# A long convolution and a cosine-gated MLP on one core: sines of tables, stores of matrices and a copy moved in their queues

## The chip, the cores and the metric

One core of a Trainium2 chip. It has five engines that run their own instruction queues in order: TensorE (PE; its weight loads are listed as PEld), VectorE (DVE), ScalarE (ACT), GpSimd (POOL) and SyncE (SP, which here only issues DMAs). They wait for each other by semaphores, and an instruction that waits holds up everything behind it on its own engine. The metric is device microseconds of one execution; the kernel before takes 3782.1 us (median of four runs, 3780.03 to 3782.74).

## The reference

```
B, S, D = 4, 12480, 128
h_filt = (relu(pos_emb @ w1) @ w2) * exp(-0.01 * pos)[:, None]
u = x * v
y = causal convolution of u with h_filt along S      # by FFT of length 2*S
X = (x * y).reshape(B*S, D)                           # 49920 rows
h = X @ w_in                                          # 128 -> 2048
out = (h * cos(h)) @ w_out                            # 2048 -> 128
```

All is float32 (w_in and w_out come as 64-bit floats and are converted on the chip).

## The kernel before, in words

**Convolution.** It is a transform of length M = 96 x 120, in two steps each way, by matmuls with tables of cosines and sines. For each batch there are four stages: f1 (64 units of two channels: matmuls against the table `c1`, L404, then copies out of PSUM, L420 to L422 and L414, done for some units by ACT and for the others by DVE, after a fixed share); f2 (48 units of two frequencies: matmuls with a matrix `w`, L445, then the product with the filter's transform `h` on DVE, L464 or L468/L470, whose sums POOL takes, L471); i1 (64 units: matmuls with the table `cs`, L476, a copy on ACT, L484, and a sum and a difference on DVE, L486); i2 (30 groups of four matrices `tm`, L501, then a product with x on DVE, L506, which is stored to `zd`).

The filter goes through f1 as well (evictions L431 to L436 and L412/L414), and through f2 together with batch 0 (`f2_both_units`; its matmuls are L448 and L451). In that stage the matrix w(j) of each unit is made from the tables `even` and `tw_w`: ACT writes one term to a PSUM bank (L291), DVE adds the other (L293). SP stores it to `wd` (L613), since the later batches load it again; the filter's product h(j) is made by ACT (L624) and stored to `hd` (L626) for the same reason. w has two buffers, h three. `units` (L524) gives the order: in unit j come w(j+1), then the matmuls of unit j, then h(j-1), its store and the product of unit j-1.

**Tables.** `inverse_tables` (L252) makes ten pieces of the tables `cs`, `rows` and `tw_t` beside the filter's f1. POOL works out the arguments (L200 to L217), ACT takes their sine (L226). A sine is issued when four arguments are waiting, the rest after the last; then SP stores the three tables (L270). The loop at L860 advances this by one piece at every fifth step of f1 (a unit of f1 has two steps).

**Conversions.** `beside` (L870) runs the conversion of the 64-bit weights beside f1 of batch 0 (w_in) and beside i1 of batch 0 (w_out), eight pieces each, one at every 14 steps. A piece takes DVE (L133, L141, L151), POOL (L135, L137, L147, L156) and ACT (L144, L146). In i1, `some_groups` also makes the matrices of six of the 30 groups, one matrix at every fifth step; at its end it starts the first i2 (`next(backs[0])`), which makes the first group `tm`.

**Groups.** A matrix of a group is made by `turn` (L282): ACT writes a term (L291), and either DVE adds the other (L293) or ACT makes it too, in a `spare` (L296), and POOL adds (L297). Of a group's four, the first two go by DVE and the last two by POOL, with one spare. The six groups of `some_groups` go by POOL alone.

**MLP.** From 344 us on, 98 tiles of 512 columns run, each in 16 steps. A step is `moe_up` (L737 matmul to a bank `ph`, L740 ACT `a`, L743 DVE `k`, L746 POOL `f`), one step later `moe_act` (L751 ACT Sin `cs`, L753 DVE `gt`), and four steps later `moe_down` (L762, which adds up 16 steps in the bank `acc`). After the sixteenth, `moe_evict` copies the sums to `ot` on ACT (L768); `ot` goes back through transposes (L126), is copied to `ob` (L777) and stored. The convolutions of the other batches, with i2 of batch 0 first, are laced between the steps by costs written in the code (L551 to L554), until all of `zd` is there, at about 2960 us; `acc` has one bank till then.

Of the kernel before, what the change touches and what calls it, by code (L numbers as in the profile page):

```python
# [2 lines left out]

# [27 lines left out]
def kernel(  # L31
# [220 lines left out]
    def inverse_tables(pool):  # L252

        t = Tables(pool, nc.gpsimd, 4)
        part = t.whole([P, 1], [[1, 1]], channel_multiplier=1, name="part")
# [11 lines left out]
                           eighths=slice(H - 1, N2, H))  # L267
        t.finish(len(t.waiting))
        for kept, made in ((csd, cs), (rowsd, rows), (twd, tw_t)):
# [182 lines left out]

    def f2_product(pool, ps, h, k1, whole):

# [11 lines left out]
        for r, op in ((0, ALU.subtract), (1, ALU.add)):  # L466
            if not whole:
                nc.vector.tensor_tensor(y[:, r], uu[:, 0], h[:, r], op=ALU.mult)  # L468
                yield
                nc.vector.tensor_tensor(t[:, r], uu[:, 1], h[:, 1 - r], op=ALU.mult)  # L470
            nc.gpsimd.tensor_tensor(y[:, r], y[:, r], t[:, r], op=op)  # L471
            yield
# [130 lines left out]

    def f2_both_units(bank):

        with tc.tile_pool(name="both", bufs=2) as pool:
            ws = {}

            def before(j):
                ws[j] = pool.tile([KE, 2, N2], F32, name="w")  # L610
                for i in range(2):
                    make_w(ws[j][:, i, :], 2 * j + i, half=bank)
                nc.sync.dma_start(wd[j, :, :, :], ws[j][:, :, :])  # L613

            def mm(j, ps, i):
                if i == 0:
                    ps = bank(), bank()
                for filt in range(2):
                    f2_mm(ps[filt], ws[j], 2 * j, i, filt=filt == 1)
                return ps  # L620

            def after(j, ps):
                h = pool.tile([N2, 2, CB, 4], F32, name="h", bufs=3)
                nc.scalar.activation(h[:, :, :, :].rearrange("p r b j -> p (r b j)"),  # L624
                                     ps[1][0:N2, :], AF.Copy, scale=1.0 / M)
                nc.sync.dma_start(hd[j, :, :, :, :], h[:, :, :, :])  # L626
                yield from f2_product(pool, ps[0], h, 2 * j, True)

            yield from units(N1 // 2, F2_STEPS, before, mm, after, 4, ahead=1)

# [10 lines left out]

    def make_group(pool, g, t, summed, bufs=1):

        for i, n2 in enumerate(n2s(g)):
            if i < G - summed:
                make_t(t[:, i, :, :], n2)
            else:
                spare = pool.tile([N1, 2, R], F32, name="spare", bufs=bufs)
                make_t(t[:, i, :, :], n2, spare=spare[:, :, :])
            yield  # L650
        nc.sync.dma_start(td[g, :, :, :, :], t[:, :, :, :])

    def some_groups(pool):
        for g in SOME:
            t = pool.tile([N1, G, 2, R], F32, name="some", bufs=2)
            yield from make_group(pool, g, t, G, bufs=2)
        next(backs[0])

# [135 lines left out]
    with tc.manual_schedule():  # L794
        with tc.tile_pool(name="psum", bufs=8, space=PSUM) as psum, \
                ExitStack() as first:
            def bank():
                return psum.tile([P, BANK], F32, name="ps")
# [59 lines left out]
            with tc.tile_pool(name="tables", bufs=1) as pool:  # L858
                sines = inverse_tables(pool)
                for i, _ in enumerate(f1):  # L860
                    if i % 5 == 0:
                        next(sines, None)
                for _ in sines:
                    pass

# [3 lines left out]

            def beside(units, pieces, more=lambda pool: iter(())):  # L870
                with tc.tile_pool(name="convert", bufs=1) as pool:
                    convert, other = convert_units(pool, pieces), more(pool)
                    for i, _ in enumerate(units):
                        if i % 14 == 0:
                            next(convert, None)
                        elif i % 5 == 0:
                            next(other, None)
                    for _ in [*convert, *other]:
                        pass

            beside(f1_units(bank, slots[0:R, :, :, :], 0.55),
                   [(wind[:, c], w) for c, w in in_pieces])
            lpool = ctx.enter_context(tc.tile_pool(name="late", bufs=1))
            cs = third_table(lpool)
            nc.sync.dma_start(cs[:, :, :], csd[:, :, :])
            for _ in f2_both_units(bank):
                pass
# [12 lines left out]
            nc.sync.dma_start(w_in_sb[:, :], wind[:, :])  # L900
            beside(i1_units(bank), [(w_out_sb[:, c, :], w) for c, w in out_pieces], some_groups)

# [28 lines left out]
        for i in range(len(steps) + LAG):  # L931
            if i < len(steps):
# [5 lines left out]
                hidden[i] = moe_up(mpool, n, c)  # L938
            if 0 <= i - 1 < len(steps):
                gates[i - 1] = moe_act(mpool, *hidden.pop(i - 1))  # L940
            if i >= LAG:
                pn, pc = steps[i - LAG]
                moe_down(pn, pc, gates.pop(i - LAG))
                if pc == NFC - 1:
                    ots[pn] = moe_evict(mpool, pn)
            if i < len(steps):

# [39 lines left out]
```

## Time and profile before

| | |
|---|---|
| median of four runs | 3782.1 us (3780.03 to 3782.74) |
| the profiled execution, its own time | 3783.21 us |
| its span, first to last instruction | 3781.4 us |
| mean granted TensorE clock | 0.994 |
| f1 of the filter, PE | 63.1 to 113.5 us |
| f1 of batch 0, PE | 113.5 to 166.6 us |
| f2 of filter and batch 0, PE | 171.2 to 269.6 us |
| i1 of batch 0, PE | 272.6 to 333.2 us |
| i2 of batch 0 begins, PE | 338.1 us |
| first MLP matmul | 344.2 us |
| DMA | 276.14 MB, mean 73 GB/s |

A line of the profile names the source line, the engine, the operation and what it writes and reads (out<-in). In a timeline it begins with the start and the duration in us, and ends, in brackets, with the idle time of the engine just before it and what ended that. In a list of waits the three figures are us in total, number of times and the longest. The clock is the share of full speed that TensorE was granted.

### The profile page before, as it was taken

What the parts mean: (1) busy time and instruction counts of PE and PEld (TensorE: products, weight loads), DVE (VectorE), ACT (ScalarE), POOL (GpSimd) and SP (SyncE); (2) the same over time, 40 slices, a digit from 0 to 9 for tenths busy, and PEclk for the clock granted to TensorE, in tenths of its full rate; (3) what the DMA queues carried; (4) which work ended last, traced back from release to release, by engine and by line L of the source; (5) the groups of instructions that cost most, each with busy time, mean ns of one, the idle gap of its engine ahead of it and who ended that gap; (6) DMA issues with size and microseconds to landing.
All of it is one profiled execution on the core that took longest, in us unless ns stands there. A gap on an engine that the chain in (4) does not pass through costs nothing.

```text
span 3781.4 us, 47199 instructions
## 1 busy us (share of the span) xinstructions
PE 3700.1 (98%) x13546; PEld 2107.6 (56%) x13546; DVE 2762.4 (73%) x5562; ACT 2520.6 (67%) x4683; POOL 2594.1 (69%) x2342
## 2 busy tenths in 40 slices
PE   7898999999999999999999999999999999999999
PEld 6777555655466555555565556555566544444444
DVE  7887887688766777778767786788765566666666
ACT  5757776766665557766655567666664677777777
POOL 7667886588854665688745664788644577777776
PEclk9999999999999999999999999999999999999999
DMA  5263451022202550122103540122105200000000
GB/s 166 65 183 107 151 150 51 19 73 77 72 18 74 180 151 27 36 76 79 57 18 111 177 121 21 48 79 75 41 12 167 87 21 19 17 21 19 17 21 14
DMA packets 209498, 276.14 MB, mean 73 GB/s; under 512 B 17111, under 2 KB 146535, under 8 KB 209111
## 3 DMA queue, kind: packets, MB, share of 16 engines
q1 hardware_dynamic: 209239, 273.12, 24.5%
q8 instruction: 109, 1.79, 0.2%
q14 instruction: 150, 1.23, 0.1%
HBM read 193.64 MB, written 79.42 MB: 72 GB/s over the span
## 4 chain that ended last, share of the span: by engine, by line
PE 83%; POOL 6%; DVE 3%; DMA 3%; ACT 3%; issue 2%; SPq 0%; POOLq 0%; DVEq 0%; ACTq 0%
PE ph L737 31%; PE acc L762 27%; PE cv L762 5%; PE cv L501 4%; PE cv L476 4%; POOL f L746 4%; PE cv L404 3%; PE cv L445 3%; PE ph L126 2%; DMA hd<-h 2%; PE ps L404 2%; POOL tm L297 1%; ACT cs L751 1%; DVE k L743 1%; PE ps L476 1%
## 5 line engine op out<-in xcount | busy, mean ns | idle before, releaser
L746 POOL TENSOR_TENSOR f<-a,k 128x512 f32<-128x512 f32 (+1 forms) x1568 | 1988.8, 1268 | 1049.3 <-DVE k L743 1049.0
L737 PE MATMUL ph<-at,w_in_sb 128*128 128x512 f32 (+1 forms) x3136 | 1597.9, 591 | 6.4 <-DVE gt L753 5.8
L740 ACT ACTIVATE a<-ph,quarter 128x512 f32<-128x512 f32 (+1 forms) x1568 | 1073.3, 684 | 752.0 <-PE ph L737 742.3
L762 PE MATMUL acc<-gt,w_out_sb 128*128 128x512 f32 (+1 forms) x2688 | 1373.6, 592 | 9.3 <-ACT ot L768 8.9
L753 DVE TENSOR_TENSOR gt<-ph,cs 128x512 f32<-128x512 f32 (+1 forms) x1568 | 1077.2, 687 | 319.8 <-ACT cs L751 291.6
L743 DVE TENSOR_SCALAR k<-a 128x512 f32<-128x512 f32 (+1 forms) x1568 | 768.4, 490 | 618.9 <-ACT a L740 602.2
L751 ACT ACTIVATE cs<-f 128x512 f32<-128x512 f32 (+1 forms) x1568 | 980.5, 625 | 335.8 <-POOL f L746 333.5
L762 PEld LDWEIGHTS acc<-gt,w_out_sb 128*128 128x128 f32 x2688 | 505.5, 189 | 661.7 <-issue 618.4
L737 PEld LDWEIGHTS ph<-at,w_in_sb 128*128 128x128 f32 x3136 | 553.1, 190 | 338.6 <-issue 265.7
L471 POOL TENSOR_TENSOR slots<-slots,t 120x256 f32<-120x256 f32 x384 | 311.7, 818 | 58.7 <-DVE t L464 25.9
L501 PEld LDWEIGHTS cv<-slots,tm 96*104 96x104 f32 x1920 | 239.1, 170 | 110.5 <-issue 84.9
L501 PE MATMUL cv<-slots,tm 96*104 96x128 f32 x1920 | 253.4, 274 | 11.3 <-DVE tm L293 4.9
L762 PE MATMUL cv<-gt,w_out_sb 128*128 128x512 f32 (+1 forms) x448 | 224.5, 583 | 0.7 <-DVE gt L753 0.7
L476 PEld LDWEIGHTS cv<-cs,slots 120*96 120x96 f32 x1536 | 177.5, 168 | 68.2 <-issue 66.3
L476 PE MATMUL cv<-cs,slots 120*96 120x120 f32 x1536 | 183.8, 266 | 0.0
L445 PE MATMUL cv<-slots,w 124*120 124x256 f32 x576 | 173.0, 380 | 0.0
L445 PEld LDWEIGHTS cv<-slots,w 124*120 124x120 f32 x576 | 103.6, 184 | 123.8 <-issue 111.1
L404 PEld LDWEIGHTS cv<-c,slots 104*124 104x124 f32 x768 | 132.5, 192 | 71.2 <-issue 58.3
L404 PE MATMUL cv<-c,slots 104*124 104x192 f32 x768 | 151.2, 326 | 4.8 <-DVE gt L753 3.5
L762 PEld LDWEIGHTS cv<-gt,w_out_sb 128*128 128x128 f32 x448 | 84.9, 190 | 104.5 <-issue 99.5
L392 DVE TENSOR_TENSOR xt<-xt,vt 104x256 f32<-104x256 f32 x177 | 138.2, 788 | 1.0 <-DMA vt<-in_v_dram 1.0
L486 DVE TENSOR_TENSOR slots<-cv,other 96x240 f32<-96x240 f32 x384 | 133.6, 394 | 4.2 <-ACT other L484 4.2
(129 smaller groups left out, 2569.6 us busy)
## 6 DMA issues: line engine op xcount, KB each, us to landing
h<-hd SPq DMA_DIRECT2D x144, 240.0 KB
tm<-td SPq DMA_DIRECT2D x96, 312.0 KB
xt<-in_x_dram SPq DMA_DIRECT2D x120, 208.0 KB
vt<-in_v_dram SPq DMA_DIRECT2D x120, 208.0 KB
xs<-in_x_dram SPq DMA_DIRECT2D x120, 208.0 KB
zd<-zs SPq DMA_DIRECT2D x119, 208.0 KB
zb<-zd SPq DMA_DIRECT2D x96, 256.0 KB
w<-wd SPq DMA_DIRECT2D x144, 116.2 KB
```

The lines of the kernel that those rows point to most:

```text
L404: nc.tensor.matmul(ps[0:KE, i * 2 * N1:(i + 1) * 2 * N1], u[:, b, 0:KE, i], c1[0:u.shape[0], :, :].rearrange("p r k -> p (r k)"), start=Tr ...
L445: nc.tensor.matmul(pi, w[:, i, :], parts[0:KE, :, k], start=True, stop=True)
L471: nc.gpsimd.tensor_tensor(y[:, r], y[:, r], t[:, r], op=op)
L476: nc.tensor.matmul(ps[0:N1, (i * 2 + r) * N2:(i * 2 + r + 1) * N2], parts[0:N2, r, :, b, i], cs[:, r, :], start=True, stop=True)
L501: nc.tensor.matmul(ps[0:R, i * D:(i + 1) * D], t[:, i, r, :], slots[0:N1, :, place, :], start=(r == 0), stop=(r == 1))
L737: nc.tensor.matmul(ph[:, 0:m], w_in_sb[:, c * P:(c + 1) * P], ats[n][:, 0:m], start=True, stop=True)
L740: nc.scalar.activation(a[:, 0:m], ph[:, 0:m], AF.Identity, bias=quarter[:, 0:1], scale=INV_TWO_PI)
L743: nc.vector.tensor_scalar(out=k[:, 0:m], in0=a[:, 0:m], scalar1=ROUND, scalar2=ROUND, op0=ALU.add, op1=ALU.subtract)
L746: nc.gpsimd.tensor_tensor(f[:, 0:m], a[:, 0:m], k[:, 0:m], op=ALU.subtract)
L751: nc.scalar.activation(cs[:, 0:m], f[:, 0:m], AF.Sin, scale=TWO_PI)
L753: nc.vector.tensor_tensor(gt[:, 0:m], ph[:, 0:m], cs[:, 0:m], op=ALU.mult)
L762: nc.tensor.matmul(accs[n][:, 0:m], w_out_sb[:, c, :], gt[:, 0:m], start=(c == 0), stop=(c == NFC - 1))
```

## The change

Seven edits:

1. The tables' sines are held until all ten arguments have been issued (`lag` 4 to 11, twelve buffers for them), and are then issued one at each fourth step. The loop goes on into f1 of batch 0 until the tables are stored.
2. Conversions beside f1 come every 10 steps, beside i1 every 12, and the extra matrices at steps 1 and 5 of each nine.
3. `w` gets its own pool, and w(0) is made before what is left of f1 of batch 0. From w(2) on its store is issued after the store of h.
4. In the last unit of the filter's f2, DVE takes the sums of the product instead of POOL.
5. The first i2 is started ahead of the last of the six extra groups.
6. A group's matrices alternate between DVE and POOL, with two spares everywhere.
7. In an MLP step `moe_down` and `moe_evict` are issued ahead of `moe_act`; of these only `ot` (ACT) shares an engine with a moved instruction, the Sin.

```diff
-        t = Tables(pool, nc.gpsimd, 4)
+        t = Tables(pool, nc.gpsimd, 11)
...
-        t.finish(len(t.waiting))
+        while t.waiting:
+            t.finish(1)
+            yield
         for kept, made in ((csd, cs), (rowsd, rows), (twd, tw_t)):
             nc.sync.dma_start(kept[:, :, :], made[:, :, :])
...
-    def f2_product(pool, ps, h, k1, whole):
+    def f2_product(pool, ps, h, k1, whole, sums=nc.gpsimd):
...
-            nc.gpsimd.tensor_tensor(y[:, r], y[:, r], t[:, r], op=op)
+            sums.tensor_tensor(y[:, r], y[:, r], t[:, r], op=op)
...
-    def f2_both_units(bank):
+    def f2_both_units(bank, w_pool):
+        ws, unkept = {}, []
+        def before(j):
+            ws[j] = w_pool.tile([KE, 2, N2], F32, name="w")
+            for i in range(2):
+                make_w(ws[j][:, i, :], 2 * j + i, half=bank)
+            unkept.append(j)
+            if j < 2:
+                keep_w()
+        def keep_w():
+            while unkept:
+                k = unkept.pop(0)
+                nc.sync.dma_start(wd[k, :, :, :], ws[k][:, :, :])
...
+        def after(j, ps):
+            h = pool.tile([N2, 2, CB, 4], F32, name="h", bufs=3)
+            nc.scalar.activation(h[:, :, :, :].rearrange("p r b j -> p (r b j)"),
+                                 ps[1][0:N2, :], AF.Copy, scale=1.0 / M)
+            nc.sync.dma_start(hd[j, :, :, :, :], h[:, :, :, :])
+            keep_w()
+            yield from f2_product(pool, ps[0], h, 2 * j, True,
+                                  nc.vector if 2 * j + 2 == N1 else nc.gpsimd)
+        steps = units(N1 // 2, F2_STEPS, before, mm, after, 4, ahead=1)
+        yield next(steps)
         with tc.tile_pool(name="both", bufs=2) as pool:
...
+            yield from steps
...
-    def make_group(pool, g, t, summed, bufs=1):
+    def make_group(pool, g, t, summed):
         for i, n2 in enumerate(n2s(g)):
-            if i < G - summed:
+            if summed < G and i % 2 == 0:
                 make_t(t[:, i, :, :], n2)
             else:
-                spare = pool.tile([N1, 2, R], F32, name="spare", bufs=bufs)
+                spare = pool.tile([N1, 2, R], F32, name="spare", bufs=2)
...
-            yield from make_group(pool, g, t, G, bufs=2)
-        next(backs[0])
+            yield from make_group(pool, g, t, G)
+            if g == SOME[-2]:
+                next(backs[0])
...
-                for i, _ in enumerate(f1):
-                    if i % 5 == 0:
-                        next(sines, None)
-                for _ in sines:
-                    pass
+                first_f1 = f1_units(bank, slots[0:R, :, :, :], 0.55)
+                for i, _ in enumerate(chain(f1, first_f1)):
+                    if i % 4 == 0 and next(sines, "made") == "made":
+                        break
...
-            def beside(units, pieces, more=lambda pool: iter(())):
+            def beside(units, pieces, every, more=lambda pool: iter(())):
...
-                        if i % 14 == 0:
+                        if i % every == 0:
                             next(convert, None)
-                        elif i % 5 == 0:
+                        elif i % 9 in (1, 5):
                             next(other, None)
...
-            beside(f1_units(bank, slots[0:R, :, :, :], 0.55),
-                   [(wind[:, c], w) for c, w in in_pieces])
+            w_pool = first.enter_context(tc.tile_pool(name="w", bufs=2, side="right"))
+            f2 = f2_both_units(bank, w_pool)
+            next(f2)
+            beside(first_f1, [(wind[:, c], w) for c, w in in_pieces], 10)
...
-            beside(i1_units(bank), [(w_out_sb[:, c, :], w) for c, w in out_pieces], some_groups)
+            beside(i1_units(bank), [(w_out_sb[:, c, :], w) for c, w in out_pieces], 12, some_groups)
...
-            if 0 <= i - 1 < len(steps):
-                gates[i - 1] = moe_act(mpool, *hidden.pop(i - 1))
             if i >= LAG:
                 pn, pc = steps[i - LAG]
                 moe_down(pn, pc, gates.pop(i - LAG))
                 if pc == NFC - 1:
                     ots[pn] = moe_evict(mpool, pn)
+            if 0 <= i - 1 < len(steps):
+                gates[i - 1] = moe_act(mpool, *hidden.pop(i - 1))
```

## The prediction, before the changed kernel had run

> **What bounds the kernel now.** I read the busy shares first, then the windows by stage, then the waits of PE inside each, and the timeline around each wait.
>
> ```profile
> PE 3700.1 (98%) x13546; PEld 2107.6 (56%) x13546; DVE 2762.4 (73%) x5562; ACT 2520.6 (67%) x4683; POOL 2594.1 (69%) x2342
> ```
>
> PE is busy 3700.1 of 3781.4 us, so all its idle time is 81.3 us. No edit takes a matmul away; the most to be won is part of these 81 us and what PE loses at a low clock after them. The windows (columns: stretch, length, busy us of PE, PEld, DVE, ACT, POOL with counts, granted clock, DMA share, GB/s):
>
> ```profile
> 113.50:121.50 8.00, 0.92 (x7) 0.63 (x5) 4.97 (x18) 2.12 (x9) 5.49 (x12) 0.76 0.11 33
> 121.50:166.60 45.10, 44.86 (x252) 43.94 (x252) 38.55 (x105) 38.85 (x115) 28.76 (x31) 0.93 0.22 68
> 166.60:171.20 4.60, 0.00 (x0) 0.01 (x1) 1.77 (x6) 4.49 (x16) 0.72 (x1) 0.74 0.17 50
> 171.20:175.60 4.40, 4.38 (x10) 3.36 (x11) 1.25 (x5) 1.46 (x6) 0.00 (x0) 0.50 0.19 58
> 183.40:269.60 86.20, 84.21 (x436) 65.02 (x434) 75.19 (x168) 46.72 (x123) 59.25 (x85) 1.00 0.61 179
> 269.60:273.30 3.70, 0.45 (x2) 0.26 (x2) 1.85 (x3) 0.60 (x1) 3.67 (x6) 1.00 0.65 206
> 333.20:338.10 4.90, 0.02 (x2) 0.02 (x1) 4.69 (x16) 4.33 (x14) 3.31 (x6) 0.79 0.10 27
> ```
>
> There are four holes in PE at changes of stage: 7.1, 4.6, 3.2 and 4.9 us. After the second the clock is 0.50 for 4.4 us, which costs another 2.2 us. The first hole comes from ACT standing in its queue at the last Sins of the inverse tables:
>
> ```profile
> 114.65 0.29 ACT L226 ACTIVATE rows<-turned 96x104 f32<-96x104 f32 x1 [1.74 <-POOL turned L217]
> 117.72 0.30 ACT L226 ACTIVATE tw_t<-turned 96x120 f32<-96x120 f32 x1 [2.79 <-POOL turned L217]
> 119.92 0.30 ACT L226 ACTIVATE tw_t<-turned 96x120 f32<-96x120 f32 x1 [1.89 <-POOL turned L217]
> ```
>
> PE's next matmul is at 121.44, released by an ACT copy that was behind them. From 340 us on the MoE steps run; there PE idles 32.7 us in all (a second table of windows), 15.6 of it before 614 us and 4.8 after 3500.
>
> **Part A, Sins and conversions (f1).** POOL works out the ten tables' arguments without a pause from 97.1 to 119.9; that does not change. ACT now reaches Sin k at step 40+4(k-1) of what is left, not at step 20 and on. The filter has 60 steps left, so the tenth Sin stands behind unit 9 of the next f1 stage. Without the waits PE ends the filter at about 112.4 (100 plus its 12.37 us busy to 113.5). At 0.71 us a unit, ACT is at unit 9 at 112.4+1.1+6.4 = 119.9, just as POOL is done: at most 1 us of waiting is left, and eight banks cover it.
>
> The u stage is then set by ACT: 38.85+4.49 us of its own work, five Sins of 0.30 us that fall in it, so 44.8; 2.5 us that it can't fill (it idles 6.3 there now, 3.5 of it waiting for a PE at low clock); 1.1 us to the first bank. PE alone would need 45.1 x 0.93 = 42. The conversions now come every 10 steps, five units, 3.5 us; on POOL a piece is 0.85+1.07+1.08+0.73 = 3.73, so DVE's L151 waits about 0.2 us for POOL at each of eight pieces, 1.6. The first f2 matmul moves from 171.2 to 112.4+1.1+44.8+2.5+1.6 = 162.4. w(0) is made ahead, so 0.5 of the 0.8 us from the last eviction (170.4) to that matmul goes too. That is 8.8+0.5, less 1.0 left for the Sins: **-8.3**. If the first raw piece (its memory is free only when the three table stores land) comes 2 us late, or the POOL lag is double, it is -5; if ACT fills all its gaps, -12.
>
> PE would still wait some 2 us ahead of f2. Rows: after 1.29 us idle (303.7) the clock stays 1.00, after 3.06 us (269.6) it is 0.64 over the next 4.7 us. Two us lies between; I keep the old loss, with 2.2 us as the bound of the gain.
> The Trainium skill, "TensorE: Matmul & The Clock Gate", Part 1: The HAM clock gate, says that a window of about 3.4 us idle drops the clock to half; by it 2 us would cost nothing and the sum would be 2.2 us lower, though 3.06 us already cost something here.
>
> **Part B, f2's stores.** Per unit, SP issues the store of w(j+1), then that of h(j-1). ACT waits for h's store (35.3 us in 38 waits), and the chain of waits is made of it. I do not believe the chain. h(9) is written at 191.83 and read by DVE only after w(11), at 193.7; nothing else waits for it. What PE waits for is w:
>
> ```profile
> 191.85 0.24 SPq L613 DMA_DIRECT2D wd<-w  x1
> 195.36 0.59 DVE L293 SCALAR_TENSOR_TENSOR w<-even,tw_w,ps 124x120 f32<-124x120 f32 x2 [0.34 <-DMA wd<-w]
> 195.75 0.69 PE L445 MATMUL ps<-slots,w 124*120 124x256 f32 x2
> ```
>
> w has two buffers: made (0.59), stored at +0.62, landed after 3.1 (179.58) to 4.1 us (250.89), mostly 3.35, then overwritten. Two units take 0.62+3.35+0.05 = 4.02, so 2.01 each, which is the measured step; while the buffers were fresh (177 to 182) it was 1.74. The new order puts w's store behind h's. In the steady state h(j-1) is done 0.2 us after w(j)'s store is issued and 1.8 us ahead of w(j+1), so the pairs on the queue come as before, and w's round trip is untouched: **0** for 44 units (bounds -12, all at 1.74, and +3 if h's data ahead of w's adds 0.14 us a trip).
> The Trainium skill, "DMA: Bandwidth & Descriptors", Anatomy of one DMA, fits 2.0 us plus bytes over 436 GB/s (for the other descriptor path); 116.2 KB would be an estimated 2.3 us, the w loop 1.5 us a unit, h the bound and this edit worth the whole 12 us; the landings above speak against it.
>
> The last unit's two sums go to DVE. POOL ends them at 273.3 as numbers five and six of a backlog of 4.16 us. DVE ends t(47) at 271.73; two sums of 0.43 (DVE's L398 at 104x256) end at 272.5, POOL's other four at 271.9: **-0.6** (0 to -1).
>
> **Part C, i1 and the first group.** The first tm group is made at step 91, not after the last. PE's 4.9 us hole ends with DVE tm at 338.08, but i2 also needs the last i1 sums, which DVE ends near 337.7: what is late next is only 0.4 us earlier. Clustering the conversions (every 12 steps) lets DVE run them down by step 108, so that its tail loses one L151 (0.41) and its wait on ACT; against it, POOL needs 3.73+2.67x0.62 = 5.4 us per 12 steps in place of 5.1 of PE. I take **-1.5**, from +3 (POOL late by 0.4 us for eight pieces) to -4.9.
>
> **Part D, the copy ahead of the Sin.**
>
> ```profile
> PE acc L762 <- ACT ot L768: 8.9, 14, 1.5
> 385.59 0.63 ACT L751 ACTIVATE cs<-f 128x512 f32<-128x512 f32 x1 [0.88 <-POOL f L746]
> 386.12 0.49 ACT L768 COPY ot<-acc 128x416 f32<-128x416 f32 x1
> 386.66 1.13 PE L762 MATMUL acc<-gt,w_out_sb 128*128 128x512 f32 x2 [0.64 <-ACT ot L768]
> ```
>
> The copy frees the one acc bank; now it stands behind a Sin that waits for POOL. PE's order is unchanged. Each of the 14 waits (1.5 at most) is shorter than or about the Sin and its wait, so they go. Four us of the 8.9 lie after 614, where little else stops PE: 3.5. The 4.9 before it are in the stretch where POOL sets the pace (219.5 of 255 us busy), so less than half, 2.0: **-5.5** (-9 to -2). The Sin starts some 0.57 us later, once in 16 steps; four steps of gt buffers cover that. What is queued behind it on ACT is the next `a`.
>
> **Part E, groups by turns.** The same matrices by the same engines, two spares: ACT's 6.6 us of waits for a spare (11 times) go, POOL's two adds are parted by a DVE one. In the POOL-paced stretch I take **-1** (-3 to +2, an add meeting DVE: L297 takes 0.61 to 1.77).
>
> **Sum.** 8.3+0+0.6+1.5+5.5+1 = 16.9 off the profiled execution's 3783.2 us (span 3781.4 and 1.8 around it): 3766.3, so **3766**; the median of the four runs, 3782.1, is 1.1 lower, within their spread. A measurement tells about 0.2% (7.6 us) from no change.
>
> **Rivals.** (1) The chain is right and h's store held f2: 44 x 0.27 = 12 us more, 3754. For it: 35.3 us of waits; against: h's slack of 1.3 us. Chance 0.12. (2) The stalls only move: conversions at 3.5 us outrun POOL, DVE and ACT wait in their queues in f1 and i1, C is +3, A -5, and in the POOL-paced stretch D gives 2: about 3777, within 0.2%. For it: POOL's 3.73 and 5.4 us above. Chance 0.15. (3) Slower: in all 98 tiles the Sin behind the copy reaches PE through gt, 0.57 us each, 56 us: 3822. It decides against the change from some 30 tiles on (16.9/0.57). Against: PE waits for gt only about 12 us in the whole run, nearly all before 614. Chance 0.05. The forecast has 0.68 (3757 to 3774).
>
> Faster by over 0.2%: 0.68+0.12 = 0.80; within: 0.15; slower: 0.05. The range takes in (1) and (2): 3753 to 3778.
>
> **What would show it.** Right: no ACT wait at L226 over 1 us; first L445 near 162; f2 units still 2.01 us with DVE w waiting for wd, though ACT's wait at L624 is gone; PE's wait for ot near 0. Wrong: f2 units near 1.75 (then 1), L151 waiting for POOL (then 2), PE waiting for gt at tile ends after 614 (then 3).

## The result and the profile after

The changed kernel takes 3777.7 us (median of 32 runs, 3772.77 to 3784.21) beside 3783.11 us of the kernel before on the same chips (50 runs): the ratio is 0.9986, with a 95% interval of 0.9981 to 0.9991. That is 5.4 us less, where 16 were predicted; by the prediction's bound of 0.2% it counts as no change, though the interval leaves out 1. The profiled execution has a span of 3778.2 us (own time 3780.25).

The first part of its page, columns as before the change:

```profile
PE 3700.6 (98%) x13546; PEld 2110.8 (56%) x13546; DVE 2781.1 (74%) x5564; ACT 2518.7 (67%) x4683; POOL 2571.3 (68%) x2340
```

PE's work is the same; the span lost 3.2 us. The windows by stage: two of f1, its end, f2's start and i1's end (stretch, length, busy us of PE, PEld, DVE, ACT, POOL, granted clock, DMA share, GB/s):

```profile
116.30:123.20 6.90, 3.16 (x17) 2.57 (x17) 6.66 (x20) 4.23 (x14) 3.28 (x8) 0.87 0.10 29
123.20:165.00 41.80, 38.48 (x212) 36.74 (x212) 36.32 (x94) 33.06 (x96) 32.00 (x32) 0.94 0.26 79
165.00:168.60 3.60, 0.02 (x1) 0.00 (x1) 1.84 (x6) 3.52 (x12) 0.00 (x0) 1.00 0.14 33
168.60:173.00 4.40, 4.37 (x13) 3.37 (x14) 1.61 (x5) 2.07 (x7) 0.00 (x0) 0.61 0.09 27
...
336.90:340.20 3.30, 0.20 (x3) 0.04 (x1) 3.30 (x11) 2.37 (x7) 0.00 (x0) 0.94 0.00 0
```

The first hole of 7.1 us is gone, but f1 now has waits all along (3.3 us of the 41.8 in the second line), and the three other holes are still there, though shorter: 3.6 us ahead of f2, 2.7 ahead of i1 and 3.1 ahead of i2. Lines have moved by 1 to 9 in the first half of the file and by 15 in the MLP (L226 is L227, L293 is L296, L624 is L633, L762 is L777). The longest wait of a Sin in ACT's timeline:

```profile
118.00 0.30 ACT L227 ACTIVATE tw_t<-turned 96x120 f32<-96x120 f32 x1 [1.73 <-POOL turned L218]
```

The three waits there fell from 6.4 us to 3.3 (0.72, 1.73, 0.85). Where did the rest go? The table has the marks that all profiles share, in us from the span's start (some kernels are told below; up to 344 us `d_alone` is the kernel before, so the first two rows show how far one profile differs from the next: 1 to 2 us).

| profile | f2's first matmul | first h | i1's first matmul | i2's first | batch 1's f1 | span |
|---|---|---|---|---|---|---|
| before | 171.22 | 175.04 | 272.65 | 338.08 | 610.56 | 3781.4 |
| d_alone | 169.48 | 173.20 | 270.69 | 336.15 | 609.84 | 3770.2 |
| after | 168.63 | 171.97 | 270.97 | 340.19 | 618.03 | 3778.2 |
| x_conv14 | 165.55 | 172.25 | 272.37 | 341.68 | 615.82 | 3777.3 |
| x_noc | 167.70 | 170.13 | 270.83 | 336.27 | 613.46 | 3774.9 |
| x_nob | 167.58 | 171.15 | 268.11 | 337.25 | 610.54 | 3771.9 |
| x_pace | 163.80 | 170.53 | 271.04 | 337.21 | 611.46 | 3772.8 |
| x_cs | 165.08 | 171.87 | 270.94 | 336.60 | 610.53 | 3770.8 |
| x_da | 169.78 | 173.68 | 271.80 | 338.28 | 610.52 | 3770.5 |
| x_last | 166.94 | 170.76 | 268.91 | 334.29 | 609.19 | 3768.3 |

From before to after: f2 begins 2.6 us earlier and i1 1.7, i2 begins 2.1 later, batch 1's f1 7.5 later, and from there to the end 10.7 us are won. The first three differences are hardly more than two profiles of the same instructions differ by; the last two are clear of it. So one part seems to pay more than all that was predicted for it, and the rest together to cost.

### The profile page after: what moved, and what is told of

It is laid out like the page before. It is cut to its first block, busy times and chain, and to the rows that moved or that the text cites. A ratio compares the mean times of both kernels' runs of the same rounds, so it can differ in the third digit from the quotient of the medians.

```text
span 3778.2 us, 47196 instructions
## 1 busy us (share of the span) xinstructions
PE 3700.6 (98%) x13546; PEld 2110.8 (56%) x13546; DVE 2781.1 (74%) x5564; ACT 2518.7 (67%) x4683; POOL 2571.3 (68%) x2340
## 4 chain that ended last, share of the span: by engine, by line
PE 86%; DVE 3%; POOL 2%; DMA 2%; ACT 1%; issue 1%; POOLq 0%; DVEq 0%; SPq 0%; ACTq 0%
PE ph L752 33%; PE acc L777 28%; PE cv L777 5%; PE cv L504 5%; PE cv L479 4%; PE cv L448 3%; PE cv L407 3%; PE ph L127 2%; POOL f L761 2%; PE ps L448 1%; DMA tm<-td 1%; PE ps L479 1%; ACT cs L766 1%; DVE gt L768 1%; DVE slots L489 1%
## 5 line engine op out<-in xcount | busy, mean ns | idle before, releaser
L752 PE MATMUL ph<-at,w_in_sb 128*128 128x512 f32 (+1 forms) x3136 | 1601.8, 592 | 8.3 <-DVE gt L768 7.4
L777 PE MATMUL acc<-gt,w_out_sb 128*128 128x512 f32 (+1 forms) x2688 | 1370.0, 591 | 0.0
L758 DVE TENSOR_SCALAR k<-a 128x512 f32<-128x512 f32 (+1 forms) x1568 | 796.5, 508 | 552.2 <-ACT a L755 536.7
L777 PEld LDWEIGHTS acc<-gt,w_out_sb 128*128 128x128 f32 x2688 | 508.3, 189 | 643.0 <-issue 631.7
L752 PEld LDWEIGHTS ph<-at,w_in_sb 128*128 128x128 f32 x3136 | 553.5, 190 | 343.2 <-issue 261.1
L777 PE MATMUL cv<-gt,w_out_sb 128*128 128x512 f32 (+1 forms) x448 | 224.5, 583 | 0.7 <-DVE gt L768 0.7
L777 PEld LDWEIGHTS cv<-gt,w_out_sb 128*128 128x128 f32 x448 | 84.9, 190 | 104.4 <-issue 99.5
```

The lines of the kernel that those rows point to most:

```text
L752: nc.tensor.matmul(ph[:, 0:m], w_in_sb[:, c * P:(c + 1) * P], ats[n][:, 0:m], start=True, stop=True)
L758: nc.vector.tensor_scalar(out=k[:, 0:m], in0=a[:, 0:m], scalar1=ROUND, scalar2=ROUND, op0=ALU.add, op1=ALU.subtract)
L777: nc.tensor.matmul(accs[n][:, 0:m], w_out_sb[:, c, :], gt[:, 0:m], start=(c == 0), stop=(c == NFC - 1))
```

## The experiments

Theory at the start: the copy ahead of the Sin is worth more than 5.5 us and the other parts lose. Rival: the other parts give what was predicted, and the copy does not. Each ratio below is to the kernel before, on the same chip, with its 95% interval (3 to 5 us to each side, 2 for the whole change).

### The copy alone, and without it

`d_alone`, the kernel before with only this:

```diff
-            if 0 <= i - 1 < len(steps):
-                gates[i - 1] = moe_act(mpool, *hidden.pop(i - 1))
             if i >= LAG:
...
                     ots[pn] = moe_evict(mpool, pn)
+            if 0 <= i - 1 < len(steps):
+                gates[i - 1] = moe_act(mpool, *hidden.pop(i - 1))
```

> The kernel before with one edit: the copy of a tile's sums (ot) is issued ahead of the Sin. Theory: this edit alone holds the gain of the MLP, and it is larger than the 5.5 us predicted, because the weight load of the next tile's first acc matmul waits for ot too (40.3 us in 46 waits of PEld, against 8.9 us in 14 waits of PE), which opens a gap of about 0.27 us between matmuls that PE's idle time does not show. Expected: tile starts gain 0.2 to 0.4 us a tile between tiles 9 and 63, 8 to 12 us in all, about 3772; PE's and PEld's waits for ot near 0. Rival: the gain after 614 us comes from elsewhere in the change (groups by turns, other phases of the queues), and this edit gives the 4 us of the waits after 614 or less, 3778 to 3780.

Measured: 3772.84 us, 0.997 (0.9958 to 0.9981): 11.6 us less, twice what the whole change gives. `x_nod` is the changed kernel with the same lines put back.

> The changed kernel with the Sin put back in front of the copy of a tile's sums, as before the change; the other four parts stay. The copy alone gave 11.6 us (3784.5 to 3772.8) and the whole change 5.4, so by sums the other parts together cost about 6. Theory: the parts add up, and this kernel takes 3783.1 + 6 = 3789 us (3786 to 3792), slower than before. Rival: the copy is worth less beside the other parts, since the MLP is held by something else there; then this kernel is at 3780 to 3784, no slower than before.

Measured: 3788.48 us, 1.0012 (1.0003 to 1.002). The parts add up, as the theory had it: without the copy the change makes the kernel slower.

Where does it come from? The lists of waits, first of before, then of d_alone (us in total, times, longest):

```profile
PEld acc L762 <- ACT ot L768: 40.3, 46, 2.3
PE acc L762 <- ACT ot L768: 8.9, 14, 1.5
```

```profile
PEld acc L762 <- ACT ot L768: 8.2, 27, 1.1
PE acc L762 <- ACT ot L768: 0.3, 1, 0.3
```

The prediction read the second line of before alone. The first one is a weight load that waits while the matmul ahead of it still runs by the model, so PE shows no idle time. The timeline of before at the end of a tile (some rows of ACT and PE):

```profile
905.72 0.63 ACT L751 ACTIVATE cs<-f 128x512 f32<-128x512 f32 x1 [0.37 <-POOL f L746]
905.75 1.02 PE L737 MATMUL ph<-at,w_in_sb 128*128 128x512 f32 x2
906.26 0.57 ACT L768 COPY ot<-acc 128x512 f32<-128x512 f32 x1
906.88 0.30 PEld L762 LDWEIGHTS acc<-gt,w_out_sb 128*128 128x128 f32 x2 [0.93 <-ACT ot L768]
906.88 1.13 PE L762 MATMUL acc<-gt,w_out_sb 128*128 128x512 f32 x2
```

The same place in after:

```profile
912.29 0.58 ACT L783 COPY ot<-acc 128x512 f32<-128x512 f32 x1
912.52 1.02 PE L752 MATMUL ph<-at,w_in_sb 128*128 128x512 f32 x2
912.77 0.63 ACT L766 ACTIVATE cs<-f 128x512 f32<-128x512 f32 x1
913.38 1.02 PE L777 MATMUL acc<-gt,w_out_sb 128*128 128x512 f32 x2
```

From L737's start to L762's, which begins with its weight load, it is 1.13 us, from L752's to L777's 0.86. The matmul before the waiting one is drawn to 906.77, so PE's row has 0.11 us of idle time, less than the 0.27 that the step lost. I took this step, start to start, less its 0.86, wherever the matmul begins just behind the copy: before has 14.3 us of it in 30 tiles, x_nod 13.6 in 28, d_alone 1.0 in 2, after 0.1 in 1. Half of it (7.0 in before) lies in the first seven tiles, where POOL sets the pace, and no gain shows there: from the first MLP matmul to batch 1's f1, d_alone takes 267.9 us and before 266.3. The other 7.3 us are after that, where d_alone gains 10.5. Most of the rest is in the next step. The weight load that waited is not hidden beside a matmul, so the two matmuls of L762 take 1.13 us in before and 1.02 in after. Measured to L762's second matmul (1.29 us where nothing waits), the loss after batch 1's f1 is 10.1 us in before and 9.4 in x_nod, and nothing in d_alone and after; 0.5 of before's is a fall of the clock in one tile (last section).

### Groups by turns

`e_alone` (before, with the turns and the two spares), and `x_noe` (after, with these lines put back):

```diff
-            if i < G - summed:
+            if summed < G and i % 2 == 0:
...
-                spare = pool.tile([N1, 2, R], F32, name="spare", bufs=bufs)
+                spare = pool.tile([N1, 2, R], F32, name="spare", bufs=2)
```

> The kernel before with one edit: a group's four matrices by turns on DVE and POOL, with two spares. In the changed kernel the stretch of i2 of batch 0 (first MLP matmul to the first f1 matmul of batch 1) is 271.0 us long against 266.4 before. Theory: the turns cost this, because POOL's add of the last matrix now ends nearer to the matmuls that read it (PE waits 2.4 us for POOL tm there, DVE's adds reach later); expected here: the stretch is 3 to 5 us longer and the kernel 3785 to 3788. Rival: the turns are harmless or gain 1 us as predicted, and the stretch got longer by the start of the pipeline or by the copy ahead of the Sin; expected then 3781 to 3783 with the stretch at 265 to 267.

> The changed kernel with a group's matrices made as before (the first half of a group on VectorE, the second half on GpSimd, one spare; two in the groups beside i1). Theory: the turns are what lengthens the stretch from the first MLP matmul to batch 1's f1, 271.0 us in the changed kernel and 266.3 before; here it comes back to 266 to 268, and the whole to 3773 to 3775 us. Rival: the turns cost nothing (alone, on the kernel before, they measured 1.0001), and the stretch is long because i1 hands it other work; then the stretch stays at 270 or more and the whole at 3777 to 3778.

Measured: 3785.07, 1.0001 (0.9992 to 1.0009), and 3777.93, 0.9982 (0.9973 to 0.9991). The stretch from the first MLP matmul to batch 1's f1 is 269.7 us in e_alone (266.3 before) and 269.8 in x_noe (271.0 after). By the times the turns cost nothing that can be told, and x_noe's theory fell. The intervals of 3 us do not tell the 1 us that was predicted from nothing either.

### i1's companions

`x_step10` keeps the extra matrices away from i1's first ten steps, `x_noc` puts both of i1's paces and the place of the first group back, `x_i1conv` only the conversions', `x_i1mat` only the matrices' (in both the first group stays early):

```diff
-                        elif i % 9 in (1, 5):
+                        elif i % 9 in (1, 5) and i > 9:
```

```diff
-            if g == SOME[-2]:
-                next(backs[0])
+        next(backs[0])
...
-                        elif i % 9 in (1, 5):
+                        elif i % 5 == 0:
...
-            beside(i1_units(bank), [(w_out_sb[:, c, :], w) for c, w in out_pieces], 12, some_groups)
+            beside(i1_units(bank), [(w_out_sb[:, c, :], w) for c, w in out_pieces], 14, some_groups)
```

> The changed kernel, with the extra matrices beside i1 begun at step 10 in place of step 1. In the changed kernel ACT stands 6.6 us at the first of them, since the load of tw_t lands only at 275.4; DVE then idles 5.0 us for ACT's copies. Theory: this wait is what made i1 3.8 us longer (270.97 to 340.19, against 65.4 us before); expected: i1 64 to 66 us, i2 begins 3 to 5 us earlier, about 3774. Rival: i1 is longer because conversions every 12 steps and the matrices ask too much of POOL and DVE, whatever the first wait; then i1 stays at 68 to 70 us and the time within 1 us of the changed kernel's.

> The changed kernel with i1's companions as before: conversions every 14 steps, a matrix every 5th, the first group after the last of the five. Theory: i1's 3.8 us more (65.7 in the three kernels without this part, 69.5 in seven with it) are its pace: i1 at 65 to 66, the gap to i2 about 5 us as before, the first i2 matmul and the MLP 2 to 4 us earlier, the whole at 3774 to 3776. Rival: i1 is long because tw_t comes late for the first matrices (6.6 us of ScalarE's wait) and because f2 ends otherwise; i1 stays at 68 or more and the whole at 3777.

> The changed kernel with only the conversions beside i1 at every 14 steps (the matrices stay two in nine). If the conversions' pace is what lengthens i1, it falls from 69.5 to 66 and the whole to 3775; if the matrices' is, it stays at 68.5 to 70 and the whole at 3777 to 3778.

> The changed kernel with only the matrices beside i1 at every fifth step (the conversions stay at 12, the first group early). If the matrices' pace is what lengthens i1, it falls from 69.5 to 66 and the whole to 3775; if the conversions' is, it stays at 68.5 to 70 and the whole at 3777 to 3778. If both are needed, both kernels are at 67 to 68.

| | time | ratio | from i1's first matmul to i2's, us |
|---|---|---|---|
| after | 3777.7 | 0.9986 (0.9981 to 0.9991) | 69.2 |
| x_step10 | 3779.11 | 0.9985 (0.9976 to 0.9994) | 68.3 |
| x_i1conv | 3780.97 | 0.9988 (0.9979 to 0.9997) | 68.0 |
| x_i1mat | 3777.57 | 0.9982 (0.9974 to 0.9991) | 68.1 |
| x_noc | 3774.54 | 0.9975 (0.9965 to 0.9986) | 65.4 |
| before | 3783.11 | 1 | 65.4 |

i1 takes 68.3 to 70.2 us in the nine profiles that have this part and 65.4 to 66.5 in the nine that do not. Two of its waits in after, between 270 and 341 us:

```profile
PE ps L479 <- DVE slots L489: 9.0, 9, 1.6
ACT some L294 <- DMA tw_t<-twd: 6.6, 1, 6.6
```

The same first line in x_noc:

```profile
PE ps L479 <- DVE slots L489: 4.6, 5, 1.6
```

ACT stands at the first matrix until tw_t lands; keeping the matrices away (x_step10) gives back about 1 us of the 3.8. PE also waits longer for evictions on DVE. From first to last, i1's own matmuls take 66.1 us in after, 64.0 in x_i1conv, 63.7 in x_i1mat and 60.6 in x_noc, so either pace has a share of some 2 us and neither alone is the cause. The hole behind them is 3.1 us in after and 4.9 in x_noc: the first group made early gains 1.8 us there, as meant, and the paces cost three times as much. No run moves the first group alone.

### f1's conversions, and where their gain goes

`x_conv14` is after with this, `x_pace` the same with i1's companions and the groups as before:

```diff
-            beside(first_f1, [(wind[:, c], w) for c, w in in_pieces], 10)
+            beside(first_f1, [(wind[:, c], w) for c, w in in_pieces], 14)
```

> The changed kernel with the conversions beside f1 every 14 steps as before the change, where it has 10. In its f1 the evictions on ScalarE stand behind a conversion's sig, which waits for VectorE and GpSimd, 8 pieces at GpSimd's 4.2 to 4.4 us, and TensorE waits for such evictions in 5 pieces, 3.3 us, between 143 and 160 us, and 3.6 at its end. Theory: the closer conversions eat what the Sins gave; at 14 f1 is 53 to 55 us (57.5 in the changed kernel), f2 starts at 164 to 166, the whole is at 3773 to 3775. Rival: f1's own evictions (VectorE and ScalarE over 90 per cent busy from 128 to 160 us before the change) set it, and f1 stays at 57 and the whole at 3777.

> The changed kernel with both paces and the groups as before: conversions every 14 steps beside f1 and i1, a matrix every 5th, a group's first half on VectorE; what stays is the Sins beside the first matmuls of f1, the stores of f2 in their new order with w's first units early, the last sums on VectorE, and the copy ahead of the Sin. By sums of the parts (4 from f1, 3 from i1 to the MLP, 2 from the stretch behind it, taken off 3777.7): 3769 us, and so 2 to 5 below the copy alone (3772.8). Rival: the parts hand their waits on to one another, and it is at 3772 to 3775.

Measured: x_conv14 3777.02 us, 0.9986 (0.9977 to 0.9994); x_pace 3772.93, 0.9971 (0.996 to 0.9983). f1 is 53.3 and 52.2 us, where after has 57.7: the conversions' pace was what ate the Sins' gain. This is a piece in after's f1 (POOL's, DVE's and ACT's rows of the conversion):

```profile
139.14 1.07 POOL L138 TENSOR_SCALAR power<-power 128x256 uint32<-128x256 uint32 x1
140.25 0.42 DVE L152 SCALAR_TENSOR_TENSOR power<-raw,power 128x256 uint32<-128x256 uint32 x1 [0.51 <-POOL power L138]
140.29 0.96 POOL L148 TENSOR_TENSOR sig<-sig,low 128x256 f32<-128x256 f32 x1
140.59 0.82 DVE L134 TENSOR_SCALAR power<-raw 128x256 uint32<-128x256 uint32 x1
...
141.70 0.42 ACT L145 ACTIVATE sig<-sig 128x256 f32<-128x256 uint32 x1 [1.42 <-DVE sig L142]
...
143.31 1.07 POOL L138 TENSOR_SCALAR power<-power 128x256 uint32<-128x256 uint32 x1
```

POOL does not stop between the rows that are left out, and a piece takes it 4.17 us (139.14 to 143.31), while ten steps of f1 were set down as 3.5. DVE waits for POOL, ACT for DVE, and f1's evictions stand behind both. POOL's add takes 0.96 us here (0.73 in before, where it runs apart from DVE's L151 and L133), and DVE's L134 beside it 0.82 (0.28 there). The Trainium skill, "SBUF — State Buffer", section "SBUF: two separate sides", has GpSimd and some VectorE forms share one pair of ports under an exclusive lock; that L134 ends 0.16 us behind POOL's add agrees with it, though no run here shows which forms of DVE are meant.

But the whole gains little or nothing (x_pace came out as its rival had it): f2 is 106.8 and 107.2 us, and i1 begins at 272.4 and 271.0. The wait of x_pace's first h, and SP's own rows:

```profile
ACT h L633 <- DMA wind<-power: 4.9, 1, 4.9
```

```profile
159.62 8.54 SPq L159 DMA_DIRECT2D wind<-power  x3
170.57 0.34 SPq L900 DMA_DIRECT2D cs<-csd  x1
170.96 0.30 SPq L622 DMA_DIRECT2D wd<-w  x1
```

The last converted piece's store is issued at 168; h, which does not read that piece, waits for it to land, since it takes its place in memory. So does cs, whose load holds the stores behind it in SP's queue. The first h is at 170 to 172 us in x_conv14 and x_pace as in after, whenever f1 ends. Two kernels part the causes: `x_cs` (x_pace with cs's load behind f2's fourth unit) and `x_pace12` (x_cs with f1's conversions every 12 steps).

```diff
-            nc.sync.dma_start(cs[:, :, :], csd[:, :, :])
-            for _ in f2:
-                pass
+            for i, _ in enumerate(f2):
+                if i == 16:
+                    nc.sync.dma_start(cs[:, :, :], csd[:, :, :])
```

> The kernel x_pace with cs's load issued after f2's fourth unit. There f2 starts at 163.8, but its third w waits to 174.3 us for the store of w's second unit, which left SyncE at 171.0, behind cs's load (170.6), and h waits to 170.5 for the last store of a converted piece. Theory (queue): the stores of w leave at 167 and the third w is made 1.5 to 2.5 us earlier, f2 at 104.7 to 105.7 us (107.2), the whole at 3771. Rival (place in memory): h's wait to 170.5 stays, VectorE stands behind it, and f2 stays within 0.7 us of 107.2.

> x_cs with f1's conversions every 12 steps, so that the last one is stored some 4 us before f1's end in place of 5 us behind it. Theory (place in memory): h then waits for nothing, f2 starts at 164 to 166 us and takes 101 to 103 us, i1 starts at 266 to 268 (271.0 in x_pace), and the whole is at 3768 to 3770, below the copy alone (3772.8). Rival: GpSimd (4.2 us a piece) is outrun again, TensorE waits in f1 as in the changed kernel, f2 starts at 167 or later, and the whole is at 3772 or more.

Measured: x_cs 3771.36 us, 0.9963 (0.9951 to 0.9976); x_pace12 3771.13, 0.9963 (0.9949 to 0.9976). In x_cs f2 is 105.9 us, between the two expectations and 1.4 less than in x_pace, and h still waits 5.0 us for the last piece: the queue has a part, and the place in memory still holds h; which is the larger is not shown. In x_pace12 that wait is gone, but f1 is 56.3 us: POOL is outrun again, and f2 begins at 168.0, as its rival had it. Either way i1 begins at 271 to 272.

### The Sins without the rest

`x_da`: before, with the copy and edit 1 (Sins held, issued beside f1), the conversions at 14.

```diff
-        t = Tables(pool, nc.gpsimd, 4)
+        t = Tables(pool, nc.gpsimd, 11)
...
-                for i, _ in enumerate(f1):
-                    if i % 5 == 0:
-                        next(sines, None)
-                for _ in sines:
-                    pass
+                first_f1 = f1_units(bank, slots[0:R, :, :, :], 0.55)
+                for i, _ in enumerate(chain(f1, first_f1)):
+                    if i % 4 == 0 and next(sines, "made") == "made":
+                        break
...
-            beside(f1_units(bank, slots[0:R, :, :, :], 0.55),
+            beside(first_f1,
```

> The kernel before with two parts of the change: the copy ahead of the Sin, and the Sins beside the first matmuls of f1; the conversions stay at 14. Theory: f1 and what is ahead of it gain what the first piece's 7.1 us wait and the clock of 0.51 in the 8 us behind it cost before, some 5 us by f2's start (171.2 before, 168.2 on average in the changed kernels), and the whole is at 3767 to 3769, below the copy alone (3772.8). Rival: the Sins only move the wait from one piece into several, and the whole is at 3772 to 3773.

Measured: 3770.65 us, 0.9966 (0.9953 to 0.9978), beside 0.997 for the copy alone: not to be told from it. PE ends f1 at 159 and waits 10.4 us for w, whose memory here is also the last piece's; f2 begins where it did.

### f2's stores

`x_even` stores the constant `even` where w was stored, so that w's buffers wait for no store (the later batches then load another matrix than w). `x_half` stores half of each h, and the later batches load that half twice. `x_hq` issues h's store from ACT's queue. `x_nob` is after with w's store ahead of h's again.

```diff
-                nc.sync.dma_start(wd[k, :, :, :], ws[k][:, :, :])
+                nc.sync.dma_start(wd[k, :, :, :], even[:, :, :])
```

```diff
-                nc.sync.dma_start(hs[j][:, :, :, :], hd[j, :, :, :, :])
+                for r in range(2):
+                    nc.sync.dma_start(hs[j][:, r, :, :], hd[j, :, 0, :, :])
...
-            nc.sync.dma_start(hd[j, :, :, :, :], h[:, :, :, :])
+            nc.sync.dma_start(hd[j, :, 0, :, :], h[:, 0, :, :])
```

```diff
-            nc.sync.dma_start(hd[j, :, :, :, :], h[:, :, :, :])
+            nc.scalar.dma_start(hd[j, :, :, :, :], h[:, :, :, :])
```

```diff
-            if j < 2:
-                keep_w()
+            keep_w()
...
             nc.sync.dma_start(hd[j, :, :, :, :], h[:, :, :, :])
-            keep_w()
```

> The changed kernel, in which the 48 stores to wd read the constant table even (same shape and size) and not w, so that the traffic and its place in SP's queue stay but no buffer of w waits for its store; the later batches therefore load another matrix than w. Theory: the round trip of w's store through two buffers sets f2's 2.01 us a unit; expected: 1.74 to 1.80 us a unit, f2 10 to 12 us shorter (102.3 to about 91), about 3766. Rival: the store of h, or DMA throughput, or DVE's own work sets the step; then 1.95 to 2.01 us a unit and no gain.

> The changed kernel storing only the first half (r = 0) of each filter product h in the first f2, 120 KB a unit where it was 240, and the later batches load that half twice, so their products differ. In the kernel before, in the changed one and in the one without w's round trip, f2 goes at 2.01 us a unit with 356 KB stored a unit, 177 to 182 GB/s in every stretch from 184 us on. Theory: that rate of the stores is f2's limit, and whichever buffer is short shows it; with 236 KB a unit the limit falls to 1.3 us and VectorE's own 1.74 us (the step of the first units before) takes over: f2 (102.3 us) at 88 to 91, the whole at 3764 to 3767. Rival: the step is the loop of w on VectorE and its four pairs of matmuls (0.39 + 1.56 + 0.05 us), and f2 stays at 101 to 102.

> The changed kernel with the first f2's store of h issued by ScalarE's queue in place of SyncE's, the same bytes. If f2's 2.01 us a unit is the rate of one queue (the DMA engines are 60 per cent busy meanwhile), two queues lift it: f2 at 88 to 92 us and the whole at 3764 to 3768. If it is the rate of the memory or of the engines for such rows, f2 stays at 101 to 102 and the whole at 3777. If ScalarE's issues hold up its own queue (some 0.1 us each in 50 units), f2 is 2 to 5 us longer.

> The changed kernel with w's store issued as soon as w is made, ahead of h's, as before the change; all else is left. Theory: behind h's store the first w's land late (f2's first steps are 3.2, 2.1, 3.0, 2.2, 2.8 us in the changed kernel, 4.3, 2.2, 1.8, 1.8, 2.1 before), and the order costs about 2 us: from the first h to i1's first matmul 97.5 to 98.3 us (99.0 in the changed kernel), i1 at 269 to 270, the whole at 3775 to 3776. Rival: the new order is neutral, since 356 KB a unit leave at the same rate either way; 99 to 101 us, and the whole at 3777 to 3778.

Measured: x_even 3777.37 us, 0.998 (0.9971 to 0.9989), f2 101.6 us; x_half 3770.92, 0.9968 (0.9955 to 0.998), f2 97.1; x_hq 3789.11, 1.0015 (1.0006 to 1.0024), f2 112.2; x_nob 3775.99, 0.9979 (0.9971 to 0.9988), f2 100.5.

In x_even DVE no longer waits for a store, and after the first ten units, most of them of some 1.74 us, a unit still takes 2.01 us: the prediction's step, that w's round trip sets it, fell. The list of waits of before already spoke against it (172 to 268 us): DVE's w waits far more often for PE than for the store.

```profile
DVE w L293 <- PE ps L445: 7.4, 31, 0.6
DVE w L293 <- DMA wd<-w: 2.4, 5, 0.9
```

What waits in x_even is h (the same stretch):

```profile
ACT h L633 <- DMA hd<-h: 33.0, 36, 1.4
```

With half of h's bytes most units take between 1.71 and 2.1 us, 1.92 on average from the eleventh step on, where after has 2.05 by the same count: neither the 1.74 of the theory nor the rival's step of before. So the bytes stored (178 to 181 GB/s between 184 and 266 us in before, after and x_even) are a part of f2's limit; what the rest is stays open. A second queue made it worse, by more than the third case that was written down; there DVE waits 15.8 us for w's stores, in 12 waits of up to 2.3, and an issue takes ACT 0.32 us where 0.1 was set down. Which of these costs the 9.9 us is not shown.

The order of the two stores is settled better. DVE's third to seventh w in after (every second one shown):

```profile
171.99 0.59 DVE L296 SCALAR_TENSOR_TENSOR w<-even,tw_w,ps 124x120 f32<-124x120 f32 x2 [2.55 <-PE ps L451]
...
177.13 0.59 DVE L296 SCALAR_TENSOR_TENSOR w<-even,tw_w,ps 124x120 f32<-124x120 f32 x2 [1.16 <-PE ps L448]
...
182.13 0.59 DVE L296 SCALAR_TENSOR_TENSOR w<-even,tw_w,ps 124x120 f32<-124x120 f32 x2 [1.01 <-DMA wd<-w]
```

and the third and seventh in x_nob:

```profile
171.17 0.59 DVE L296 SCALAR_TENSOR_TENSOR w<-even,tw_w,ps 124x120 f32<-124x120 f32 x2 [2.78 <-PE ps L451]
...
178.79 0.59 DVE L296 SCALAR_TENSOR_TENSOR w<-even,tw_w,ps 124x120 f32<-124x120 f32 x2 [0.21 <-ACT h L632]
```

The same four steps take 10.1 us in after and 7.6 in x_nob. Behind h's store w's lands late while the buffers are fresh; later both orders run at 2.01. From the first h to i1's first matmul eleven profiles with the new order take 99.0 to 100.9 us, six with the old one 97.0 to 98.1, and x_even 97.8 (x_half and x_hq, with other bytes or another queue, are left out). The new order costs some 2 us, about what the Sins win ahead of it.

### What gains, together

`x_last`: the copy, the Sins, w(0) early and the last sums on DVE; the stores, the groups and i1's companions as before, f1's conversions at 12.

> The copy ahead of the Sin, the Sins beside f1, w's first unit early and the last sums on VectorE; the stores, the groups and i1's companions as before the change, f1's conversions every 12 steps. By the parts: 3772.8 for the copy alone, less 2 for the Sins where the order of the stores doesn't take it back: 3770 to 3771, with i1's first matmul at 269 to 270.5 (271.9 on average in the kernels with the old order). Rival: f1's conversions at 12 hold GpSimd as at 10 and the whole is at 3772 to 3774.

Measured: 3770.91 us, 0.9964 (0.995 to 0.9977), i1's first matmul at 268.9, both as expected or a little better. It beats both kernels, and so do x_cs, x_pace12 and x_da (0.9963 to 0.9966); they can't be told from each other, nor with certainty from the copy alone (0.997).

## Why the prediction was off

The sign was right and the time was that of the second rival (3777), but by luck: its sum has 2 us for the copy, where 11.6 came, and 5 for f1, where 2.6 came at most. Its mechanism, conversions that outrun POOL while DVE and ACT wait in their queues, did come.

- **Part A (predicted -8.3) failed at the step "the first f2 matmul moves from 171.2 to 162.4".** The Sins' half held: POOL was done at 120, and ACT's waits halved. The half with the conversions did not: a piece is 4.17 us of POOL, not 3.73. Of the 0.44 us between them, 0.21 are the gaps between POOL's four instructions (3.96 us of work in the piece shown), which the sum left out, and 0.23 come from POOL's add, which now meets DVE's instructions. DVE's waits for POOL and ACT's for DVE at the conversions came to 2.1 and 4.2 us (124 to 165 us) where 1.6 was set down. From f1's first matmul to f2's it stayed at 57.7 us, and f2 began at 168.6. A second step was only implied, that what f2's start gains reaches f2's end. x_conv14 shows that it doesn't: f2's start moved by 3.1 us more and i1's did not.
- **Part B (0): the bound of +3 was nearer.** The steady 2.01 us held, and the first rival (12 us more from h's store) did not come: ACT's waits for hd are gone and the step stayed. But the working looked only at the steady state; the first units lose some 2 us (x_nob). The reason given for 2.01, w's round trip, fell (x_even): it rested on one row that waits for wd, and 31 of DVE's waits there are for PE against 5 for the store.
- **Part C (-1.5, bound +3): it was about +4** (x_noc, and the length of i1 in 18 profiles). The row for it stood in the prediction: POOL 5.4 us a piece against 5.1 of PE. I set it against a gain at the tail. That gain came (1.8 us off the hole ahead of i2). But the bound of +3 counted POOL alone: i1's matmuls take 5.5 us more, and PE waits 9.0 us for DVE's evictions where it waits 4.6 in x_noc.
- **Part D (-5.5, bounds -9 to -2): it was -11.6**, the term that was most mis-sized. Two steps failed: only PE's idle rows were counted (8.9 us), not the 46 waits of a weight load, and half of the early wait was taken for a gain where none shows. What the runs show is 10.1 us lost at tile ends after batch 1's f1 in before and none with the copy ahead; the prediction had 3.5 for all that lies there.
- **Part E (-1): not to be told from 0**, inside its bounds.

Together: the copy gives 11 us; i1's companions take 4 of it back, the stores' order 2, the groups perhaps 1, and f1's gain of 2 to 3 us remains: some 6 in all, and 5.4 was measured. Only the copy's term is clear of the noise by its times; the small ones rest on the marks of profiles. The third rival, the Sin behind the copy, did not come: of ACT's Sins only that one in 16 is later, and PE's weight loads wait less for gt than before (25.6 us in 70 waits, 36.3 in 121 before).

## What to carry to other kernels

Count waits of weight loads too, and measure a lost step from start to start: the idle time of a matmul row is less than the step loses, and the matmul behind a late weight load is late as well. A stage that starts earlier is worth nothing until it is known what its first buffers wait for (here memory that the stage before still uses, and a queue's order). Work that is laced beside a stage at an even pace should be paced by the slowest engine's whole piece, with the neighbours it will meet, and not by the free time on average.

## What the runs showed of the hardware

Short holes can cost clock. The windows that follow the changed kernel's holes of 2.68 and 3.10 us in PE (the granted clock is the column behind the busy times; the one after the hole of 3.61 us stands above, with 0.61):

```profile
271.00:275.60 4.60, 4.60 (x27) 4.48 (x28) 0.26 (x2) 0.11 (x1) 0.50 (x2) 0.63 0.61 194
340.20:344.50 4.30, 4.30 (x20) 4.30 (x21) 1.28 (x3) 1.21 (x4) 1.24 (x2) 0.50 0.27 78
```

In the clock records of all 20 profiles, from 60 us on, the granted clock is 0.5 or 1.0 and changes only on a beat of 3.41 us; the values above are means over stretches that hold both. It fell after beats in which PE's rows were busy for 56% or less (once 64%), and stayed at 1.0 after others of 47% and more, so the bound is near one half. What a hole costs depends on how it lies on the beat: before and x_nod have the same hole of 1.46 us in PE at one tile end (before at 2686.37 us, x_nod at 2693.63). In before its beat is 44% busy and the clock is 0.5 for the next one, in x_nod 57%, and it stays at 1.0.

The Trainium skill, "TensorE: Matmul & The Clock Gate", Part 1, speaks of an idle window of about 3.4 us. The beat agrees with its length, but a hole need not fill it: those of 2.68 and 3.10 us are shorter and the clock fell all the same, so the measurement decides.

With the stores of w and h from two queues (x_hq) f2 took 112.2 us, where it took 102.3 from one queue, and the core's DMA moved 161 GB/s between 184 and 266 us where it moved 180; with one queue the DMA engines were 60% busy.
